# Feed-forward weights loaded by ranges of their 2048 columns, and the second product of two blocks in partial sums

## The chip, the cores and the metric

The kernel runs on one core of a Trainium2 chip. The metric is device time in microseconds (us) of one execution; the time before is the median of three runs. TensorE (PE) does matrix products, VectorE (DVE) and ScalarE (ACT) do elementwise work and read PSUM, GpSimd (POOL) does elementwise work in SBUF, and SyncE (SP) issues all DMAs, in one queue and in order.

## What is computed

Attention with pooled queries, then a gated feed-forward layer:

```python
q_pool = q.reshape(4, 8, 576, 2, 64).mean(axis=3)
attn = softmax(q_pool @ k.T / 8)          # 4 x 8 heads, 576 x 1152
x = (attn @ v), heads side by side        # 2304 rows x 512
h = x @ w_in                              # w_in 512 x 2048
g = h / (1 + exp(-h))
out = g @ w_out                           # w_out 2048 x 512
```

q, k, v, w_in and w_out are float32 (the two weights are handed over in the bit pattern of 64-bit floats, which the kernel turns into float32 by shifts and masks). Each product is done in three float16 products (high by high, high by low, low by high).

## The kernel before

**Jobs.** Attention is cut into 72 jobs, 18 for each of 4 batches: 128 pooled query rows of one pair of heads, or the last 64 rows of two pairs (ch is None). A job is scores (`scores`, L555, PE into the PSUM tiles S0 and S1), row maxima (L602, DVE), exponentials p (L618, ACT), their float16 high and low parts phl (cast L308 or L312, rest L323), a transpose of both by DMA (L641) into pt (or, for one side of the first four jobs, on PE: `turn`, L655), the product with V (`heads`, L700, into the PSUM tile po), and its scaling into x (L746, DVE). An exponential frees its S tile for the next scores.

**Blocks.** When the four pairs of a chunk are done, `rows` transposes x on PE (L771, PSUM tile px; L792 reads it) and `block` does 128 rows of the feed-forward layer; there are 18 blocks. `first(u)`, u = 0 to 3, computes 512 of the 2048 columns of h in 48 matmuls (L833) into a PSUM tile h; tanh (L847, ACT), a multiply-add (L854, DVE, which frees h), a cast and a rest give the float16 pair g[u]. `second` multiplies g by w_out in 48 matmuls (L877), one accumulation over all 16 groups of 128 columns in one PSUM tile o; one evacuation with scaling (L892, by ACT L308 or DVE L314) gives osb, which is stored. Eight g buffers hold two blocks.

**Weights.** `weights(n)`, n = 0 to 31, loads and converts 512 columns' worth of one eighth: n = 0 to 15 are w_in, 16 to 31 w_out. Each is a DMA (L455), a cast of the upper words into a PSUM tile t (ACT L308 or DVE L314, written as `mm<-wide` or `mm<-raw`), three DVE steps (L470, L478, L486, the last one frees t), a cast to the high half (`w`) and a rest to the low half (POOL, L323). The w_in pieces land in a wide SBUF buffer laid over the place where w_out will stand, so the tokens in `staged` make a w_out piece wait for the w_in pieces that lay there; the w_out pieces land in the shared pool b (12 buffers, which also hold loaded q, k, v, p, phl and pt).

**PSUM.** Of the eight banks six are S0 and S1; the tag mm has two buffers (`BUFS["mm"]`), which t, po, pp, px, h and o all share.

**Order.** A planner (`Plan.order`) simulates the engines with a cost for each step and writes out a fixed order for each engine. Attention has priorities near its job's number (the `PRI` offsets), weights near 0.95 + 0.3 n, the feed-forward matmuls 1e6 and more, so that these fill what is left:

```python
pr = 1e6 + 1000 * bid                          # block bid
"pe", 12 * pe_cost(P), lambda i=i: products(i), pr + 10 * u          # first
"pe", pe_cost(DM, DM, DM), lambda ff=ff: products(ff), pr + 100 + ff # second
w2_tokens = [x for u in range(8) for x in weight_tokens("w2", u)]
```

The last of these lines makes every step of `second` wait for the whole of w_out.

Of the kernel before, what the change touches and what calls it, by code (L numbers as in the profile page):

```python
# [53 lines left out]
FIRST_LEAD, FIRST_STEP = 2.2, 1.0  # L54
W_FIRST, W_STEP, W2_LATER = 0.95, 0.3, 0.58
V_LATER = 1.71
PRI = dict(
    score=0.07, top=-1.08, exp=-0.21, hi=0.07, lo=0.0, turn=-3.26, flip=-0.32, flat=-0.7, sums=-0.83,
    rows=0.65, side=0.2, load=-0.59, raw=-1.0,
)  # L60
EARLY, KL_EARLY, T_EARLY, WLO_EARLY, ADD_EARLY = 8, 2, False, True, True
MLP_EVAC, T_EVAC = 4.42, -1.48
BUFS = dict(w=1, slots=4, b=12, x32=2, x4=1, xt=4, g=8, t=4, small=6, S=1, mm=2)
RAW_ROOM, LOAD_ROOM, P32_ROOM, PHL_ROOM = 2, 4, 2, 0
# [5 lines left out]
AHEAD, SWITCH, STEAL = 0.78, 0.82, 1.18  # L70
# [186 lines left out]
def tile_kernel(tc, q, k, v, w_in, w_out, out):  # L257
    nc = tc.nc
    with ExitStack() as ctx:
# [3 lines left out]
        def pool(name, bufs, tags, **kw):  # L263
            pools[name] = ctx.enter_context(tc.tile_pool(name=name, bufs=bufs, **kw))
            for tag in tags:
                capacity[tag] = bufs
# [18 lines left out]
        pool("t", BUFS["t"], ["t"])  # L285
        pool("small", BUFS["small"], ["nm", "sum", "r"])
# [127 lines left out]
        def weights(n):  # L414
            name, src, scale = ("w1", w_in, W_IN_SCALE) if n < 16 else ("w2", w_out, W_OUT_SCALE)
            u, i = divmod(n % 16, 2)
            pr = W_FIRST + W_STEP * n + (W2_LATER if n >= 16 else 0)
            half = f"{name}_{u // 4}"
            if u % 4 == 0 and i == 0:
                wt[name, u // 4] = tile("w", half, [P, 4, 2, 1024], F16)  # L420
            w = wt[name, u // 4]
            if n < 16:
                half, at = n // 4, n % 4
                if at == 0:
                    wide[half] = tile("w", f"w2_{half % 2}", [P, 4, 1024], F32, "wide")
                raw = wide[half]

                def bits():
                    return raw()[:, at]
            else:  # L430
                raw = tile("b", "b", [P, S], F32, "raw", RAW_ROOM)

                def bits():
                    return raw()[:, :1024]
# [58 lines left out]
            if more != 1.0:  # L493
# [5 lines left out]
                x for a in range(2) for x in weight_tokens("w1", 4 + u // 4 * 2 + a)  # L499
# [307 lines left out]
        def block(xt, where, inputs, left=False):  # L807
# [60 lines left out]
            def second():  # L868
                o = tile("psM", "mm", [P, DM], F32)
                osb = tile("t", "t", [P, DM], F32, "osb")  # L870
                tok = ("o", bid)

                def products(ff):
                    u, e = divmod(ff, 2)
                    w = wt["w2", u // 4]()
                    for gl, wl in ((0, 0), (0, 1), (1, 0)):
                        nc.tensor.matmul(  # L877
                            o(), lhsT=g[ff // 4]()[:, gl, ff % 4],
                            rhs=w[:, u % 4, wl, e * DM : e * DM + DM],
                            start=ff == 0 and gl + wl == 0, stop=ff == 15 and gl == 1,  # L880
                        )

                w2_tokens = [x for u in range(8) for x in weight_tokens("w2", u)]
                for ff in range(16):
                    u = ff // 4
                    add(
                        "pe", pe_cost(DM, DM, DM), lambda ff=ff: products(ff), pr + 100 + ff,
                        [("ghi", bid, u), ("glo", bid, u), *w2_tokens], [tok],
                        [o, g[u], wt["w2", ff // 8]],
                    )  # L890
                either(
                    cast(DM, osb, o, 1.0 / (G_SCALE * W_OUT_SCALE)),  # L892
                    MLP_EVAC, [], [tok, ("osb", bid)], [o, osb], port=False,
                )
# [65 lines left out]
```

## Time and profile before

| | |
|---|---|
| three runs | 758.71, 764.72, 764.65 us; median 764.65 us |
| the profiled execution | 758.84 us, of which the profile's span is 757.1 us |
| busy, share of the span | PE 88%, DVE 68%, ACT 61%, POOL 58% |
| granted TensorE clock, mean | 0.96 |

Rows of the trace are given as follows. A row of stretches has its length, then each engine's busy time and its instructions, the granted TensorE clock (1.00 is 2.4 GHz, 0.50 is 1.2 GHz), the busy share of the DMA engines and GB/s. A row of waits names an instruction, what it waited for, the sum in us, how often, and the longest. A row of the timeline has start, length, engine, line, operation and count, and in brackets the idle time of the engine before it and what ended it. Times are us from the start of the span.

### The profile page before, as it was taken

To read this page: it belongs to the slowest core of one execution; us is meant where nothing else is said; L and a number is where in the kernel's file an instruction comes from. 1 tells how busy PE (TensorE), PEld (TensorE's weight loads), DVE (VectorE), ACT (ScalarE), POOL (GpSimd) and SP (SyncE) were. 2 spreads that over 40 slices of the span, in tenths; PEclk is the share of its full clock that TensorE was granted. 3 is DMA by queue.
4 is the path that set the end of the run, shared out by engine and by line. 5 is a ranking of instruction groups with operands and counts; after the bars stand their busy time and mean duration, and the time that the engine had idled before them with its cause. 6 is when DMAs were issued, how large, how long until landed. Compare 5 with 4: busy or idle time off the path is not lost. (4 is left out here: it accounts for less than half of the span.)

```text
span 757.1 us, 23661 instructions
## 1 busy us (share of the span) xinstructions
PE 664.5 (88%) x10188; PEld 478.9 (63%) x10188; DVE 518.4 (68%) x919; ACT 460.1 (61%) x678; POOL 436.7 (58%) x244
## 2 busy tenths in 40 slices
PE   1665736868989999999989999999999999999997
PEld 0343624755575868675956667777767586767874
DVE  5689898877479767766489677677668676666110
ACT  5878866785368556466567556656658465556221
POOL 4847687885126848367546564757626564848111
PEclk9868776999999999999999999999999999999999
DMA  9989988999997999999998999999998997999300
GB/s 306 221 248 241 228 190 176 190 190 175 226 285 143 157 173 150 167 159 186 211 250 172 163 141 153 166 176 205 175 278 145 154 159 151 155 172 149 58 16 14
DMA packets 346024, 133.93 MB, mean 177 GB/s; under 512 B 333376, under 2 KB 333376, under 8 KB 345920
## 3 DMA queue, kind: packets, MB, share of 16 engines
q1 hardware_dynamic: 345920, 132.43, 92.4%
q8 instruction: 79, 1.29, 0.7%
q14 instruction: 25, 0.20, 0.1%
HBM read 45.09 MB, written 4.72 MB: 66 GB/s over the span
## 5 line engine op out<-in xcount | busy, mean ns | idle before, releaser
L323 POOL TENSOR_TENSOR phl<-p,phl 128x1152 f16<-128x1152 f32 x112 | 271.6, 2429 | 153.0 <-DVE phl L312 61.0
L618 ACT ACTIVATE p<-S,nm 128x1152 f32<-128x1152 f32 x144 | 174.5, 1215 | 112.3 <-DVE nm L609 73.8
L833 PE MATMUL mm<-xt,w 128*128 128x128 f16 x3456 | 208.7, 221 | 16.6 <-DVE xt L792 4.3
L833 PEld LDWEIGHTS <-w 128*128 128x128 f16 x3456 | 198.4, 99 | 24.5 <-issue 13.2
L602 DVE TENSOR_REDUCE nm<-S 128x1 f32<-128x1152 f32 x144 | 189.6, 1349 | 30.9 <-PE S L555 30.6
L877 PE MATMUL mm<-w,g 128*128 128x512 f16 x864 | 199.4, 379 | 2.0 <-DVE t L854 0.8
L323 POOL TENSOR_TENSOR g<-t,g 128x512 f16<-128x512 f32 x72 | 93.4, 1301 | 90.6 <-ACT g L308 89.2
L700 PE MATMUL po<-V,pt 128*128 128x64 f16 (+1 forms) x4320 | 132.4, 196 | 13.8 <-DVE t L854 6.3
L700 PEld LDWEIGHTS <-pt 128*128 128x128 f16 (+1 forms) x4320 | 127.7, 103 | 24.5 <-issue 17.5
L877 PEld LDWEIGHTS <-g 128*128 128x128 f16 x864 | 79.9, 98 | 89.2 <-issue 1.9
L555 PE MATMUL S<-KH,QH 64*128 64x512 f16 (+2 forms) x480 | 90.6, 343 | 31.7 <-ACT p L618 23.5
L555 PEld LDWEIGHTS <-QH 64*128 64x128 f16 (+1 forms) x960 | 46.4, 100 | 89.7 <-issue 50.5
L308 ACT ACTIVATE phl<-p 128x1152 f16<-128x1152 f32 x86 | 99.8, 1164 | 4.3 <-issue 2.4
L854 DVE SCALAR_TENSOR_TENSOR t<-t,mm 128x512 f32<-128x512 f32 x72 | 49.2, 684 | 55.0 <-ACT t L847 53.1
L555 PE MATMUL S<-KL,QH 64*128 64x512 f16 (+2 forms) x480 | 85.7, 340 | 0.9 <-DVE KL L323 0.9
L555 PE MATMUL S<-KH,QL 64*128 64x512 f16 (+2 forms) x480 | 79.5, 339 | 0.0
L312 DVE CAST phl<-p 128x1152 f16<-128x1152 f32 x54 | 43.0, 797 | 44.7 <-ACT p L618 41.8
L847 ACT ACTIVATE t<-mm 128x512 f32<-128x512 f32 x72 | 42.6, 594 | 43.7 <-PE mm L833 43.6
L308 ACT ACTIVATE g<-t 128x512 f16<-128x512 f32 x72 | 45.4, 630 | 29.4 <-DVE t L854 29.4
L323 DVE TENSOR_TENSOR phl<-p,phl 128x1152 f16<-128x1152 f32 x28 | 49.5, 1767 | 12.8 <-ACT phl L308 12.4
L323 POOL TENSOR_TENSOR QL<-ld,QH 128x576 f16<-128x576 f32 x15 | 22.9, 1525 | 40.6 <-ACT QH L308 35.8
L746 DVE TENSOR_TENSOR x<-po,r 128x128 f32<-128x128 f32 x72 | 20.4, 284 | 30.2 <-PE po L700 30.0
(48 smaller groups left out, 460.2 us busy)
## 6 DMA issues: line engine op xcount, KB each, us to landing
ld<-v SPq DMA_DIRECT2D x16, 576.0 KB, 8.7
wide<-w_in SPq DMA_DIRECT2D x16, 512.0 KB, 5.8
raw<-w_out SPq DMA_DIRECT2D x16, 512.0 KB, 5.4
ld<-q SPq DMA_DIRECT2D x8, 576.0 KB, 6.1
ld<-k SPq DMA_DIRECT2D x8, 576.0 KB, 7.1
ld<-q SPq DMA_DIRECT2D x16, 288.0 KB, 9.5
ld<-k SPq DMA_DIRECT2D x16, 288.0 KB, 8.5
pt<-phl SPq DMA_TRANSPOSE x280, 3.6
```

The costliest lines, as they stand in the source:

```text
L308: nc.scalar.activation(out=out(), in_=src(), func=AF.Copy, scale=scale or 1.0)
L312: nc.vector.tensor_copy(out=out(), in_=src())
L323: return lambda: getattr(engine, op)(out=out(), in0=a(), in1=b())
L555: nc.tensor.matmul(o[to, c], lhsT=a[pp]()[rows, s], rhs=x[pp]()[rows, c], start=n == 0, stop=n == 2,)
L602: lambda: nc.vector.tensor_reduce(out=nm(), in_=ps()[:, :S], op=ALU.max, axis=AX.X),
L618: lambda: nc.scalar.activation(out=p32(), in_=ps()[:, :S], func=AF.Exp, scale=0.0625, bias=nm(), accum_out=sm()[:, col : col + 1],),
L700: nc.tensor.matmul(o[to, keep], lhsT=pt[:, hl * NK + c, cols], rhs=vv[:, vl, 2 * c + h], start=c == 0 and hl + vl == 0, stop=c == NK - 1 a ...
L746: lambda: nc.vector.tensor_tensor(out=to(), in0=po()[:, : 2 * D].rearrange("p (a d) -> p a d", a=2), in1=r().unsqueeze(2).to_broadcast([P, ...
L833: nc.tensor.matmul(o, lhsT=w[:, f // 2 % 4, wl, cols], rhs=moving(xl, kk), start=kk == 0 and wl + xl == 0, stop=kk == 3 and wl == 1,)
L847: lambda: nc.scalar.activation(out=t(), in_=h(), func=AF.Tanh, scale=1.0 / G_SCALE),
L854: lambda: nc.vector.scalar_tensor_tensor(out=t(), in0=t(), scalar=1.0, in1=h(), op0=ALU.add, op1=ALU.mult,),
L877: nc.tensor.matmul(o(), lhsT=g[ff // 4]()[:, gl, ff % 4], rhs=w[:, u % 4, wl, e * DM : e * DM + DM], start=ff == 0 and gl + wl == 0, stop= ...
```

## The change

The numbering of the weight pieces takes w_in and w_out in turn: pieces 0 to 3 are the first eighth of both, 4 to 7 the second, and so on; pieces 0 to 15 are the first 1024 of the 2048 columns of both weights. The wide landing buffers now lie over the place of the second halves of both, and a piece of a second half waits for all pieces of both first halves (`staged`). The second product of block 0 is done in four parts and that of block 1 in two (`PIECES`): each part has its own PSUM tile, waits only for the eighths of w_out that it uses, and stands among the steps of `first` in priority; the first part is evacuated into an SBUF tile acc, each further one is scaled and added to acc by a DVE step. The other 16 blocks keep the single accumulation. Some 20 constants of the planner are changed as well (priorities, room to be left in the buffers, switching).

```diff
--- before.py
+++ after.py
@@ -51,23 +51,24 @@
 
 WAIT = 0.1
 PREP_LEAD = 3.0
-FIRST_LEAD, FIRST_STEP = 2.2, 1.0
+FIRST_LEAD, FIRST_STEP = 0.91, 1.0
 W_FIRST, W_STEP, W2_LATER = 0.95, 0.3, 0.58
-V_LATER = 1.71
+V_LATER = 1.45
 PRI = dict(
-    score=0.07, top=-1.08, exp=-0.21, hi=0.07, lo=0.0, turn=-3.26, flip=-0.32, flat=-0.7, sums=-0.83,
-    rows=0.65, side=0.2, load=-0.59, raw=-1.0,
+    score=-0.06, top=-1.4, exp=-0.21, hi=0.27, lo=-0.34, turn=-3.17, flip=-0.32, flat=-1.01, sums=-1.89,
+    rows=0.65, side=0.26, load=-0.59, raw=-0.14,
 )
 EARLY, KL_EARLY, T_EARLY, WLO_EARLY, ADD_EARLY = 8, 2, False, True, True
-MLP_EVAC, T_EVAC = 4.42, -1.48
-BUFS = dict(w=1, slots=4, b=12, x32=2, x4=1, xt=4, g=8, t=4, small=6, S=1, mm=2)
-RAW_ROOM, LOAD_ROOM, P32_ROOM, PHL_ROOM = 2, 4, 2, 0
+MLP_EVAC, T_EVAC = 4.42, -0.66
+BUFS = dict(w=1, slots=4, b=12, x32=2, x4=1, xt=4, g=8, t=4, acc=2, small=6, S=1, mm=2)
+RAW_ROOM, LOAD_ROOM, P32_ROOM, PHL_ROOM = 2, 3, 2, 1
+PIECES = 4, 2
 BOTH_BY_PE, ONE_BY_PE, EVERY = 0, 4, 99
 
 
 LATENCY = {"pe": 0.25, "dve": 0.15, "act": 0.15, "pool": 0.15, "dma": 2.2}
 DMA_START = 1.3
-AHEAD, SWITCH, STEAL = 0.78, 0.82, 1.18
+AHEAD, SWITCH, STEAL = 0.91, 0.85, 1.18
 
 
 class Tile:
@@ -283,6 +284,7 @@
         pool("xt", BUFS["xt"], ["xt"])
         pool("g", BUFS["g"], ["g"])
         pool("t", BUFS["t"], ["t"])
+        pool("acc", BUFS["acc"], ["acc"])
         pool("small", BUFS["small"], ["nm", "sum", "r"])
         pool("psS", BUFS["S"], ["S0", "S1"], space=bass.MemoryType.PSUM)
         pool("psM", BUFS["mm"], ["mm"], space=bass.MemoryType.PSUM)
@@ -412,18 +414,17 @@
         wt, wide = {}, {}
 
         def weights(n):
-            name, src, scale = ("w1", w_in, W_IN_SCALE) if n < 16 else ("w2", w_out, W_OUT_SCALE)
-            u, i = divmod(n % 16, 2)
-            pr = W_FIRST + W_STEP * n + (W2_LATER if n >= 16 else 0)
-            half = f"{name}_{u // 4}"
+            u, which, i = n // 4, n // 2 % 2, n % 2
+            name, src, scale = (("w1", w_in, W_IN_SCALE), ("w2", w_out, W_OUT_SCALE))[which]
+            pr = W_FIRST + W_STEP * n + W2_LATER * which
             if u % 4 == 0 and i == 0:
-                wt[name, u // 4] = tile("w", half, [P, 4, 2, 1024], F16)
+                wt[name, u // 4] = tile("w", f"{name}_{u // 4}", [P, 4, 2, 1024], F16)
             w = wt[name, u // 4]
             if n < 16:
-                half, at = n // 4, n % 4
+                space, at = n // 4, n % 4
                 if at == 0:
-                    wide[half] = tile("w", f"w2_{half % 2}", [P, 4, 1024], F32, "wide")
-                raw = wide[half]
+                    wide[space] = tile("w", f"w{space % 2 + 1}_1", [P, 4, 1024], F32, "wide")
+                raw = wide[space]
 
                 def bits():
                     return raw()[:, at]
@@ -496,7 +497,7 @@
                     pr, writes=[("raw", *tok)], tiles=[raw], early=True,
                 )
             staged = [] if n < 16 else [
-                x for a in range(2) for x in weight_tokens("w1", 4 + u // 4 * 2 + a)
+                x for a in range(4) for what in ("w1", "w2") for x in weight_tokens(what, a)
             ]
             either(
                 cast(512, hi, value), pr, [("raw", *tok), *staged], [("whi", *tok)], [raw, w], early=True,
@@ -866,32 +867,51 @@
                 )
 
             def second():
-                o = tile("psM", "mm", [P, DM], F32)
-                osb = tile("t", "t", [P, DM], F32, "osb")
-                tok = ("o", bid)
-
-                def products(ff):
-                    u, e = divmod(ff, 2)
-                    w = wt["w2", u // 4]()
-                    for gl, wl in ((0, 0), (0, 1), (1, 0)):
-                        nc.tensor.matmul(
-                            o(), lhsT=g[ff // 4]()[:, gl, ff % 4],
-                            rhs=w[:, u % 4, wl, e * DM : e * DM + DM],
-                            start=ff == 0 and gl + wl == 0, stop=ff == 15 and gl == 1,
+                n = PIECES[bid] if bid < len(PIECES) else 1
+                scale = 1.0 / (G_SCALE * W_OUT_SCALE)
+                if n == 1:
+                    osb = tile("t", "t", [P, DM], F32, "osb")
+                else:
+                    osb = tile("acc", "acc", [P, DM], F32)
+                for piece in range(n):
+                    ffs = range(16 // n * piece, 16 // n * (piece + 1))
+                    o = tile("psM", "mm", [P, DM], F32)
+                    tok = ("o", bid, piece)
+
+                    def products(ff, o=o, ffs=ffs):
+                        u, e = divmod(ff, 2)
+                        w = wt["w2", u // 4]()
+                        for gl, wl in ((0, 0), (0, 1), (1, 0)):
+                            nc.tensor.matmul(
+                                o(), lhsT=g[ff // 4]()[:, gl, ff % 4],
+                                rhs=w[:, u % 4, wl, e * DM : e * DM + DM],
+                                start=ff == ffs[0] and gl + wl == 0, stop=ff == ffs[-1] and gl == 1,
+                            )
+
+                    w2_tokens = [x for u in {f // 2 for f in ffs} for x in weight_tokens("w2", u)]
+                    at = pr + 100 if n == 1 else pr + 10 * (ffs[-1] // 4) + 5
+                    for ff in ffs:
+                        u = ff // 4
+                        add(
+                            "pe", pe_cost(DM, DM, DM), lambda ff=ff, p=products: p(ff),
+                            at + 0.1 * (ff - ffs[0]),
+                            [("ghi", bid, u), ("glo", bid, u), *w2_tokens], [tok],
+                            [o, g[u], wt["w2", ff // 8]],
                         )
-
-                w2_tokens = [x for u in range(8) for x in weight_tokens("w2", u)]
-                for ff in range(16):
-                    u = ff // 4
-                    add(
-                        "pe", pe_cost(DM, DM, DM), lambda ff=ff: products(ff), pr + 100 + ff,
-                        [("ghi", bid, u), ("glo", bid, u), *w2_tokens], [tok],
-                        [o, g[u], wt["w2", ff // 8]],
-                    )
-                either(
-                    cast(DM, osb, o, 1.0 / (G_SCALE * W_OUT_SCALE)),
-                    MLP_EVAC, [], [tok, ("osb", bid)], [o, osb], port=False,
-                )
+                    if piece == 0:
+                        either(
+                            cast(DM, osb, o, scale),
+                            MLP_EVAC, [], [tok, ("osb", bid)], [o, osb], port=False,
+                        )
+                    else:
+                        add(
+                            "dve", dve_cost(DM),
+                            lambda o=o: nc.vector.scalar_tensor_tensor(
+                                out=osb(), in0=o(), scalar=scale, in1=osb(),
+                                op0=ALU.mult, op1=ALU.add,
+                            ),
+                            MLP_EVAC, [], [tok, ("osb", bid)], [o, osb], port=False,
+                        )
 
                 def store():
                     at = 0
```

## Rows read from the trace of the kernel before

**Rows 1.** Five stretches of the span, all engines.

```profile
0.00:76.00 76.00, 39.24 (x413) 25.31 (x414) 56.85 (x103) 55.57 (x81) 46.16 (x33) 0.84 0.99 254
76.00:176.00 100.00, 64.38 (x1089) 52.11 (x1087) 88.27 (x163) 73.27 (x112) 80.05 (x50) 0.85 0.97 196
176.00:230.00 54.00, 49.14 (x711) 32.83 (x710) 35.04 (x54) 28.25 (x41) 15.53 (x10) 0.97 1.01 221
230.00:700.00 470.00, 459.55 (x7307) 331.51 (x7306) 331.05 (x590) 290.41 (x426) 284.82 (x146) 1.00 1.00 173
700.00:757.00 57.00, 52.21 (x676) 37.18 (x673) 7.20 (x12) 12.59 (x21) 10.10 (x9) 0.98 0.16 30
```

**Rows 2.** The chain that ended last, from 700 us: start, length, what.

```profile
731.13 10.72 PE mm L833 x192
741.85 10.37 PE mm L877 x48
...
752.30 0.60 ACT osb L308
```

**Rows 3.** Waits of PE in the stretch 76 to 176 us.

```profile
PE S L555 <- ACT p L618: 17.0, 5, 10.8
PE po L700 <- DVE t L854: 6.3, 4, 2.1
PE mm L833 <- DVE wide L486: 3.1, 1, 3.1
PE px L771 <- DVE raw L486: 2.5, 1, 2.5
```

**Rows 4.** Timeline of POOL, 90 to 180 us, low halves of the weights.

```profile
95.55 2.47 POOL L323 TENSOR_TENSOR w<-raw,w 128x512 f16<-128x512 f32 x2
...
121.24 1.15 POOL L323 TENSOR_TENSOR w<-wide,w 128x512 f16<-128x512 f32 x1
...
175.84 1.15 POOL L323 TENSOR_TENSOR w<-raw,w 128x512 f16<-128x512 f32 x1
```

**Rows 5.** The same stretches, matmuls of the second product (L877) alone.

```profile
76.00:176.00 100.00, 0.88 (x5) 0.41 (x6) 0.85 0.97 196
176.00:230.00 54.00, 22.81 (x99) 9.04 (x98) 0.97 1.01 221
```

**Rows 6.** Timeline of PE, 94 to 180 us.

```profile
117.62 0.58 PE L555 MATMUL S<-KH,QH 64*128 64x512 f16 x1 [10.76 <-ACT p L618]
...
133.98 1.74 PE L700 MATMUL po<-V,pt 128*128 128x64 f16 x54 [1.41 <-DVE t L854]
...
157.00 2.85 PE L833 MATMUL mm<-xt,w 128*128 128x128 f16 x48
...
165.04 0.65 PE L771 MATMUL px<-one,x 128*128 128x128 f32 x4
```

**Rows 7.** Timeline of DVE, 94 to 180 us.

```profile
99.42 0.67 DVE L486 SCALAR_TENSOR_TENSOR wide<-wide,mm 128x512 uint32<-128x512 uint32 x1
...
135.75 0.29 DVE L746 TENSOR_TENSOR x<-po,r 128x128 f32<-128x128 f32 x1 [0.74 <-PE po L700]
...
160.51 0.69 DVE L854 SCALAR_TENSOR_TENSOR t<-t,mm 128x512 f32<-128x512 f32 x1 [0.65 <-ACT t L847]
```

**Rows 8.** Timeline of ACT, 88 to 128 us.

```profile
94.79 0.65 ACT L308 ACTIVATE mm<-wide 128x512 f32<-128x512 f32 x1
```

**Rows 9.** DVE's groups of instructions in 76 to 176 us: busy, mean ns.

```profile
L478 DVE SCALAR_TENSOR_TENSOR mm<-mm,raw 128x512 uint32<-128x512 uint32 x16 | 11.0, 692 | 1.1 <-ACT mm L308 0.7
...
L854 DVE SCALAR_TENSOR_TENSOR t<-t,mm 128x512 f32<-128x512 f32 x8 | 5.5, 686 | 3.3 <-ACT t L847 3.2
...
L478 DVE SCALAR_TENSOR_TENSOR mm<-mm,wide 128x512 uint32<-128x512 uint32 x7 | 4.8, 690 | 0.1
```

**Rows 10.** Shorter stretches, all engines.

```profile
95.00:114.00 19.00, 5.47 (x76) 3.93 (x74) 18.21 (x28) 11.13 (x16) 15.64 (x11) 0.77 0.84 186
114.00:133.00 19.00, 12.43 (x141) 9.26 (x141) 16.66 (x32) 13.25 (x21) 14.37 (x10) 0.68 0.91 176
```

## The prediction, made before the changed kernel had run

> **What bounds the kernel now.** First the busy shares by stretch [rows 1]. From 230 to 700 us PE works 459.55 of 470 us at a clock of 1.00, while DVE, at 331 us, is the next busiest engine: from there on the end is the sum of PE's work. Before 76 us PE idles 36.8 us, from 76 to 176 us 35.6 us, and from 176 to 230 us 4.9 us. So of the 92.6 us that PE idles, 72.4 lie ahead of 176 us, and only feed-forward work brought forward into them can shorten the whole; what is moved within the later stretches gains nothing. Next the end of the chain that ended last [rows 2]: two blocks of pure PE work, the last one 10.72 us of first product and 10.37 us of second, then an evacuation of 0.60 us. These 21.1 us a block are the unit of what can be moved, and the tail itself stays as it is (blocks 16 and 17 keep one accumulation).
>
> Then, who keeps PE idle between 76 and 176 us [rows 3]: 17.0 us are scores waiting for an exponential to free S (10.8 us in one piece), and the rest is mostly waits for whoever reads a tile of the two mm buffers last: 6.3, 3.1 and 2.5 us in the three largest such rows. Behind both stands DVE, 88.27 us busy of 100 [rows 1], with the weights' bit steps among the attention's. Last, why there is no second product in this stretch: POOL writes the last low half of w_out at 175.84 us [rows 4], and of the 864 matmuls of L877 five stand before 176 us and some hundred in the 54 us after it [rows 5]. Each step of `second` waits for all of w_out, and the eight g buffers, which hold the two blocks that are waiting, keep block 2 from starting.
>
> **The order of the weights.** The DMAs, casts, bit steps and rests are the same 32 pieces, so no engine gets less of them. What moves is what each eighth releases. Pieces 0 to 15 are now both first halves. In the trace of before the last of the first 16 pieces is done at 122.4 us (121.24 plus 1.15) and the last of all at 177.0 [rows 4]. If the pieces keep these times, columns 0 to 1023 of both weights are there by 122 us, and the third quarter (pieces 16 to 23) by about 150, halfway to the end.
>
> **The parts of the second product.** By 176 us the first three quarters of block 0 and the first half of block 1 can then be through: 36 + 24 = 60 matmuls of L877. At 48 in 10.37 us [rows 2] that is 13.0 us of PE work. Against it, `first(3)` of both blocks, which in before was done by 160 us (the last group begins at 157.00 and takes 2.85, rows 6), now needs pieces 24 to 29 and can fall behind 176: 0 to 5.7 us lost. For it the freed g buffers (block 0's first three and block 1's first two) admit block 2, whose x is transposed at 165.04 us [rows 6]: 0 to 8.6 us gained for up to three groups. These two are of the same kind and nearly the same size; I take zero for their sum and keep -5.7 to +8.6.
>
> **PSUM.** Do the parts find one of the two mm buffers free? A tile t is held from its cast at 94.79 to the end of L486 at 100.09, 5.3 us [rows 7, 8]; a tile h from 157.00 to 161.20, 4.2 us [rows 6, 7]; po from 133.98 to 136.04, 2.1 us [rows 6, 7]. From 76 to 176 us there are 16 + 7 of t and 8 of h [rows 9]; nine of po and two of px follow from the nine jobs and two chunks that end in it. With px at po's length that makes 23 x 5.3 + 8 x 4.2 + 11 x 2.1 = 179 of 200 us, an estimate that leaves 21. A part of 12 matmuls takes 2.6 us, and its reader 0.6 to 0.7 (the evacuation of rows 2; an add from PSUM and SBUF of this size is L854's 0.69, rows 9), with the hand-over some 3.6; the part of 24 takes 6.2. Three and one need 17 us. They fit barely, and only in the places where the planner's weights leave a buffer: the long idle piece before 117.62 [rows 6] is just where t's stand back to back. I take 70% of the 13.0 us as moved, 9 us; the bounds are 0 and 13.
>
> **The adds.** Block 0 has three and block 1 one, 4 x 0.69 = 2.8 us of DVE, which has 11.7 us idle of 100 here. The first part's evacuation is the one that was there. They can hold up a row maximum queued behind them on DVE, and with it an exponential and the next scores, by up to 2.8 us in all; PE's order in this stretch has idle time for that, so the cost to the end is 0 to 2.8, and I take 0. Without that idle time it would be the 2.8. The two blocks' stores to HBM follow earlier in SP's queue; the planner gives a store the priority 1e5, behind all of attention's DMAs, so I charge nothing, and without that a transpose behind it would wait for its issue.
>
> **What is late next.** With 9 us fewer of feed-forward work in stock, PE can run dry later. The place is the change of batches, where attention waits for loads of q, k and v; from 230 to 700 us PE idles 10.45 us in all [rows 1], so little is lost there now. As attention's own PE steps stand behind fewer feed-forward steps, it also comes earlier. I charge 1 us, bounds 0 and 5.
>
> **The constants.** Priorities of loads, weights and transposes shift by under two jobs, and the order of every queue with them, SP's included. A plan that is worse after 230 us can cost at most what PE then waits more; one that is better can win at most PE's 10.45 us [rows 1]. I take 0, bounds -5 and +5.
>
> **The sum.** 758.84 - 9 + 1 = 750.8 us on the profiled execution's own time (span 757.1 and 1.7 around it). That execution lies at the low end of the runs shown: their median is 5.8 us higher, and nothing in the trace says which of the two levels the changed kernel's runs will have. I give 752.
>
> **Rival: hidden.** The parts stand in the plan behind every weight step, find no mm buffer, and come out after 176 us; or they run and push back the weights by as much. Then nothing is gained but a shorter hold of o, 0 to 2 us: 757 to 759 on the profile, up to 764 at the level of the median. For it speak rows 3 and the 179 of 200 us; against it, that o's own buffer is free in the same stretch in before and that 35.6 us of PE idle are spread over all of it. The Trainium skill (Perfetto Trace Analysis, Optimization Strategy) reads repeated gaps on the engine that should be saturated as a sign that the next tile finds no room in SBUF or PSUM. The rows of waits on L854 and L486 agree for about a third of the idle time, and the 17.0 us on the exponential do not; by the rule alone this rival's time holds.
>
> **Rival: more.** All 13 us move, block 2 adds half of its 8.6, and PE's clock rises. From 95 to 133 us the granted clock is 0.77 and 0.68 [rows 10], between the two levels of 1.2 and 2.4 GHz, after and among idle stretches of PE. At these means, 46% and 64% of the time lie at the lower level; if its 5.47 and 12.43 us of work are spread alike, full clock would give back half of 2.5 + 8.0, 5 us. Together 13 + 4 + 5 = 22, less 2 for the stock: 738 to 741. Against it is that much of the idle time stays, the exponentials being late.
>
> **Rival: slower.** The new `staged` makes every piece of a second half wait for all of both first halves. In before, the first low halves out of pool b are written at 95.55 us, 25.7 us ahead of the last from the wide buffers [rows 4]. If those pieces now hold their b buffers until the first halves are through, p and phl find none, SP's queue stands with its transposes behind a load that waits for a buffer, and the weights end up to 25.7 us later, at 202. By 202 us PE has done in before the 21.4 us of two first products [rows 2] and some 12 us of second (the 0.88 us ahead of 176 and half of the 22.81 in the 54 us after it, rows 5), 33.7 together. In the changed kernel only first halves would be there: three half first products of 5.4 us and two half second products of 5.2, 26.5 together. The 7.2 us missing, and two jobs of attention held up, each with 1.74 us for po [rows 6] and about as much for its scores, 7 us, give 773, or up to 779 at the level of the median. It decides from the time at which the weights end: at 176 us those 26.5 are 4.2 more than the 22.3 of before, which then gains (11.4 + 7) / 25.7 = 0.7 us in each; so slower than before from about 182 us on. Against it: the first halves come first in every queue, and could be through before 121 if nothing of the second halves stands among them.
>
> **Chances.** Forecast 0.50 (747 to 757), hidden 0.24 (757 to 764), more 0.13 (736 to 745), slower 0.13 (768 to 780). About 1% is what a measurement of this kernel can tell from no change: 7.6 us, so faster is below 757.0, slower above 772.3. Faster: 0.50 + 0.13 = 0.63; within 1%: 0.24 and the lower end of the slower case, 0.26; slower 0.11. The range that holds 8 in 10 takes in the forecast, the hidden case and half of the larger gains, and reaches a little above the hidden case for the new plan's unknown: 740 to 766.
>
> **What would show it.** L877 matmuls in the stretch before 176 us: 60 if the forecast holds, under 15 if hidden. PE's idle time ahead of 176 us falls from 72.4 to about 63 us. The last low half of the weights ends at 170 to 182 us; later than that the slower case is in force. PE's share from 230 to 700 us stays over 97%; under 96% means that stock ran out or that the new order made waits. Waits of po and h on the last reader of an mm tile grow by no more than 5 us. The prediction would be wrong if attention, not PE, set the pace after 230 us, which idle PE at the changes of batches would show, or if the new constants moved the weights as a whole.

## The result, and the profile after

The changed kernel takes 767.25 us (median of 18 runs, 761.22 to 773.10) where the kernel before takes 759.70 us (18 runs, 758.71 to 764.72; the 764.65 known to the prediction came of three): a ratio of 1.009, 95% interval 1.007 to 1.0111. It was forecast at 752 us with a range of 740 to 766; it came out slower than the kernel before, by a little less than the 1% that the prediction takes for the least that can be told from no change. The profiled execution took 766.22 us with a span of 764.5. In its lines L487 is the weights' last DVE step (L486 before), L556 the scores, L701 po, L747 x, L834 the first product, L885 the second, L909 the add; the kernels of the experiments have small shifts of their own.

The five stretches [rows 1], with the last one 7.5 us longer:

```profile
0.00:76.00 76.00, 38.76 (x378) 24.06 (x379) 56.26 (x98) 51.50 (x74) 44.97 (x31) 0.79 0.88 228
76.00:176.00 100.00, 71.22 (x1026) 49.49 (x1026) 88.03 (x163) 70.67 (x105) 66.92 (x40) 0.88 0.99 202
176.00:230.00 54.00, 47.12 (x813) 35.67 (x814) 38.55 (x64) 33.83 (x51) 29.73 (x20) 0.97 1.02 222
230.00:700.00 470.00, 453.27 (x7240) 329.78 (x7237) 334.21 (x582) 285.77 (x421) 274.66 (x142) 1.00 0.98 174
700.00:764.50 64.50, 58.54 (x742) 40.97 (x738) 12.89 (x23) 17.17 (x28) 15.23 (x12) 1.00 0.23 44
```

The second product alone [rows 5]:

```profile
76.00:176.00 100.00, 15.65 (x60) 5.95 (x60) 0.88 0.99 202
176.00:230.00 54.00, 14.43 (x63) 5.92 (x63) 0.97 1.02 222
```

The move took place to the matmul: 60 of L885 stand between 76 and 176 us, as the prediction had it, against 5 before. PE idles 66.0 us ahead of 176 us instead of 72.4. And yet from 230 to 700 us PE idles 16.7 us instead of 10.45, and the end comes later. By the rows of stretches, PE works 511.8 us after 230 us in both kernels; it idles 22.7 us there instead of 15.2, and that difference is the 7.4 us by which the span grew. What else moved is seen in POOL's timeline, the last low half of the weights [rows 4], which ends 32 us later, at 209.1 instead of 177.0:

```profile
207.91 1.16 POOL L325 TENSOR_TENSOR w<-raw,w 128x512 f16<-128x512 f32 x1
```

and in DVE's timeline, where L747 (L746 before) ends a job of attention. Counted in the order in which they end, these are the 13th, 16th, 18th (the last of batch 0), 54th (three batches' worth), 71st and last of the 72 jobs, before:

```profile
168.88 0.29 DVE L746 TENSOR_TENSOR x<-po,r 128x128 f32<-128x128 f32 x1 [0.32 <-PE po L700]
...
192.64 0.28 DVE L746 TENSOR_TENSOR x<-po,r 128x128 f32<-128x128 f32 x1
...
208.09 0.29 DVE L746 TENSOR_TENSOR x<-po,r 128x128 f32<-128x128 f32 x1 [5.69 <-PE po L700]
...
548.64 0.29 DVE L746 TENSOR_TENSOR x<-po,r 128x128 f32<-128x128 f32 x1 [1.39 <-PE po L700]
...
702.96 0.29 DVE L746 TENSOR_TENSOR x<-po,r 128x128 f32<-128x128 f32 x1 [3.12 <-PE po L700]
...
709.76 0.29 DVE L746 TENSOR_TENSOR x<-po,r 128x128 f32<-128x128 f32 x1 [4.40 <-PE po L700]
```

and after:

```profile
161.51 0.28 DVE L747 TENSOR_TENSOR x<-po,r 128x128 f32<-128x128 f32 x1
...
201.10 0.29 DVE L747 TENSOR_TENSOR x<-po,r 128x128 f32<-128x128 f32 x1
...
214.66 0.29 DVE L747 TENSOR_TENSOR x<-po,r 128x128 f32<-128x128 f32 x1 [2.44 <-PE po L701]
...
550.83 0.29 DVE L747 TENSOR_TENSOR x<-po,r 128x128 f32<-128x128 f32 x1 [2.46 <-PE po L701]
...
709.78 0.29 DVE L747 TENSOR_TENSOR x<-po,r 128x128 f32<-128x128 f32 x1 [0.95 <-PE po L701]
...
720.63 0.29 DVE L747 TENSOR_TENSOR x<-po,r 128x128 f32<-128x128 f32 x1 [2.47 <-PE po L701]
```

Attention is 7.4 us ahead at its 13th job, then loses 16 us by the 16th, so that it is 6.6 us late at the end of batch 0. The delay does not stay as it is: 2.2 us after 54 jobs, 6.8 after 71, and 10.9 at the last job, ahead of which the new order puts 84 matmuls of first product (4.7 us on PE). For that the stretch from the last job to the end of the span is 3.5 us shorter (43.9 instead of 47.3 us); 10.9 less 3.5 is the 7.4 us between the spans. This last stretch belongs to the planned order: it is 47.2 to 47.4 us in all eight runs below that keep the order of the kernel before, and 43.9 in all three that keep that of the changed one. Within one order, the end follows attention's last job. The last block is as it was [rows 2]:

```profile
738.70 10.72 PE mm L834 x192
749.42 10.37 PE mm L885 x48
...
759.88 0.60 ACT osb L310
```

PE's waits from 76 to 176 us [rows 3] have changed hands. Two more rows of before that name the weights' last DVE step, which frees a PSUM tile, are these:

```profile
PE po L700 <- DVE wide L486: 1.7, 1, 1.7
...
PE po L700 <- DVE raw L486: 0.6, 1, 0.6
```

and after:

```profile
PE po L701 <- DVE wide L487: 7.2, 1, 7.2
PE mm L885 <- DVE raw L487: 4.9, 3, 2.3
...
PE mm L834 <- DVE t L855: 1.7, 2, 1.5
...
PE po L701 <- DVE t L855: 1.4, 1, 1.4
...
PE S L556 <- ACT p L619: 0.7, 1, 0.7
...
PE mm L885 <- DVE wide L487: 0.5, 1, 0.5
```

The 17.0 us of scores waiting for an exponential have shrunk to 0.7. The PE steps that waited for the weights' last DVE step, attention's po among them, make 12.6 us, where the four rows of this kind before make 7.9. The waits for the multiply-add, which frees the same kind of tile, fell meanwhile, from 6.3 us to 3.1 (L855 after). And the longest of these waits, 7.2 us, ends at 109.9 us, long before attention falls behind. From 161 to 201 us, where it does, PE idles 11.3 us instead of 5.9; the rows of waits there name no single releaser.

### The profile page after: what moved, and what is told of

It is laid out like the page before. It is cut to its first block, busy times and chain, and to the rows that moved or that the text cites. A ratio compares the mean times of both kernels' runs of the same rounds, so it can differ in the third digit from the quotient of the medians.

```text
span 764.5 us, 23652 instructions
## 1 busy us (share of the span) xinstructions
PE 668.9 (87%) x10188; PEld 480.0 (63%) x10188; DVE 530.0 (69%) x926; ACT 458.9 (60%) x676; POOL 431.5 (56%) x243
## 5 line engine op out<-in xcount | busy, mean ns | idle before, releaser
L834 PE MATMUL mm<-xt,w 128*128 128x128 f16 x3456 | 209.6, 220 | 15.9 <-DVE t L855 7.0
L834 PEld LDWEIGHTS <-w 128*128 128x128 f16 x3456 | 198.3, 98 | 23.6 <-issue 18.8
L885 PE MATMUL mm<-w,g 128*128 128x512 f16 x864 | 201.3, 382 | 7.1 <-DVE raw L487 4.9
L701 PE MATMUL po<-V,pt 128*128 128x64 f16 (+1 forms) x4320 | 132.2, 196 | 25.8 <-DVE wide L487 12.7
L701 PEld LDWEIGHTS <-pt 128*128 128x128 f16 (+1 forms) x4320 | 127.9, 103 | 37.3 <-issue 21.8
L325 POOL TENSOR_TENSOR g<-t,g 128x512 f16<-128x512 f32 x72 | 90.8, 1262 | 89.6 <-ACT g L310 87.8
L885 PEld LDWEIGHTS <-g 128*128 128x128 f16 x864 | 80.3, 98 | 95.8 <-issue 6.6
L556 PE MATMUL S<-KH,QH 64*128 64x512 f16 (+2 forms) x480 | 91.0, 349 | 21.9 <-ACT p L619 14.0
L310 ACT ACTIVATE phl<-p 128x1152 f16<-128x1152 f32 x88 | 101.9, 1164 | 1.1
L556 PEld LDWEIGHTS <-QH 64*128 64x128 f16 (+1 forms) x960 | 47.0, 101 | 80.1 <-issue 43.1
L855 DVE SCALAR_TENSOR_TENSOR t<-t,mm 128x512 f32<-128x512 f32 x72 | 49.3, 685 | 58.8 <-ACT t L848 57.4
L556 PE MATMUL S<-KL,QH 64*128 64x512 f16 (+2 forms) x480 | 86.7, 345 | 0.9 <-DVE KL L325 0.9
L556 PE MATMUL S<-KH,QL 64*128 64x512 f16 (+2 forms) x480 | 80.6, 344 | 0.0
L314 DVE CAST phl<-p 128x1152 f16<-128x1152 f32 x52 | 41.1, 789 | 41.2 <-ACT p L619 32.8
L325 DVE TENSOR_TENSOR phl<-p,phl 128x1152 f16<-128x1152 f32 x27 | 51.9, 1924 | 10.3 <-ACT phl L310 10.3
L556 PEld LDWEIGHTS <-QL 64*128 64x128 f16 (+1 forms) x480 | 28.9, 102 | 18.2 <-issue 5.2
L747 DVE TENSOR_TENSOR x<-po,r 128x128 f32<-128x128 f32 x72 | 20.5, 285 | 24.7 <-PE po L701 24.5
```

Source lines behind the costliest of these rows:

```text
L310: nc.scalar.activation(out=out(), in_=src(), func=AF.Copy, scale=scale or 1.0)
L314: nc.vector.tensor_copy(out=out(), in_=src())
L325: return lambda: getattr(engine, op)(out=out(), in0=a(), in1=b())
L556: nc.tensor.matmul(o[to, c], lhsT=a[pp]()[rows, s], rhs=x[pp]()[rows, c], start=n == 0, stop=n == 2,)
L701: nc.tensor.matmul(o[to, keep], lhsT=pt[:, hl * NK + c, cols], rhs=vv[:, vl, 2 * c + h], start=c == 0 and hl + vl == 0, stop=c == NK - 1 a ...
L747: lambda: nc.vector.tensor_tensor(out=to(), in0=po()[:, : 2 * D].rearrange("p (a d) -> p a d", a=2), in1=r().unsqueeze(2).to_broadcast([P, ...
```

## The experiments

Theory A is the prediction's premise: PE's sum of work sets the end. Theory B: attention's chain (scores, maximum, exponential, transposes, product with V) sets it, feed-forward work only fills the gaps, and the change has made attention of batch 0 late, through DVE's time, PSUM, the order of the weights or the planner's constants. Ratios are to the kernel before, with 95% intervals. "Order kept" means that the planned order on the engines is that of the named kernel and only the issued instructions differ; in the other runs the planner writes a new order.

**Does PE's work set the end?** Twice work was taken from PE, order kept, by leaving two of three float16 products out of some second products (the output then lacks them):

```diff
+LIGHT, LIGHT_BLOCKS = ((0, 0),), (0, 1)
...
-                    for gl, wl in ((0, 0), (0, 1), (1, 0)):
+                    for gl, wl in LIGHT if bid in LIGHT_BLOCKS else ((0, 0), (0, 1), (1, 0)):
```

Blocks 0 and 1:

> The kernel before, its order on every engine unchanged, with 64 of the 96 matmuls of the second product of blocks 0 and 1 left out (two of three float16 products): 13.8 us of PE work less between 175 and 211 us, as much as the change was to move ahead of 176. If PE's sum of work sets the end, as the prediction said: 13 us less, 746 to 748 us. If attention's own chain sets the pace from there on and the feed-forward work only fills: 0 to 4 us less, 756 to 760 us.

Measured: 759.42 us, ratio 0.9998 (0.9973 to 1.0022). 13.8 us of PE work less gain nothing. Part of it went to a lower clock, 0.81 granted from 176 to 230 us instead of 0.97, between the two levels, while PE idled more; but from 230 to 700 us the clock is 1.00 in both and PE is as busy as before (459.84 us). The attention steps behind the gap did not come sooner, and the last job of attention is where it was:

```profile
710.17 0.29 DVE L747 TENSOR_TENSOR x<-po,r 128x128 f32<-128x128 f32 x1 [4.40 <-PE po L701]
```

Blocks 9 to 12, in the stretch in which PE is busiest:

> The kernel before, its order on every engine unchanged, with two of the three float16 products of the second product left out in blocks 9 to 12: 27.6 us of PE work less between about 430 and 600 us. If PE's work sets the pace there (97 to 98% busy): 20 us less or more, 740 us. If attention's chain sets it: 0 to 5 us less, 755 to 760 us.

Measured: 763.42 us, ratio 1.0047 (1.0015 to 1.008). One row of stretches of the kernel before and one of this:

```profile
430.00:600.00 170.00, 165.45 (x2632) 118.53 (x2630) 117.94 (x208) 104.56 (x154) 97.67 (x52) 1.00 1.03 178
```

```profile
430.00:600.00 170.00, 145.57 (x2528) 111.44 (x2525) 117.43 (x206) 103.44 (x152) 98.70 (x53) 0.97 1.00 176
```

PE's busy time falls by 20 us in it, the other engines' stays, and the time is not a microsecond less. Theory A falls for the two stretches that were tested. Why this one is 0.5% slower is not known; its last job ends 4.0 us late, and from 560 to 580 us the granted clock is 0.83, between the two levels, where it was 1.00 before.

After 600 us theory A is not tested. There the kernel before shows

```profile
600.00:700.00 100.00, 99.58 (x1662) 73.50 (x1661) 66.76 (x131) 60.88 (x95) 67.73 (x34) 1.00 0.93 156
```

and its chain that ended last runs on PE alone, feed-forward steps included, from 601.5 to 670.9 us and again from 681.1 to 752.2. No run takes work out of this stretch; PE's work may well set its length. Nor does an order that is kept show what a new plan would make of freed time.

**Does the front's DVE time set it?** Two reductions of a constant tile behind L486 of pieces 8 to 31, order kept, which nothing waits for:

```diff
+                if n >= 8:
+                    for _ in range(2):
+                        nc.vector.tensor_reduce(out=spare(), in_=one(), op=ALU.max, axis=AX.X)
```

> The kernel before, its planned order unchanged, with two row maxima of a constant 128 x 128 tile added on DVE behind the last bit step of 24 weight pieces: 48 instructions of about 0.2 us, some 9 us of DVE time between 60 and 175 us that nothing waits for. If DVE's time up to the end of batch 0's attention is what that end and the whole follow: the last job of batch 0 ends 7 to 10 us later, 766 to 769 us. If DVE's idle time there (45 us by then) takes it up: 760 to 762 us.

Measured: 768.97 us, ratio 1.0125 (1.0085 to 1.0166). The 48 reductions took 282 ns each, 13.5 us in all and not some 9. The end of batch 0 and the last job:

```profile
218.05 0.29 DVE L753 TENSOR_TENSOR x<-po,r 128x128 f32<-128x128 f32 x1 [5.69 <-PE po L707]
...
722.18 0.29 DVE L753 TENSOR_TENSOR x<-po,r 128x128 f32<-128x128 f32 x1 [4.40 <-PE po L707]
```

10.0 us late at the end of batch 0, 10.9 after 54 jobs and 12.4 at the last. In the order of the kernel before, a delay of attention in front is carried through to the end, as theory B has it. Forty of the same reductions, 11.3 us, in blocks 4 to 8 (two behind each L854, order kept):

> The kernel before, its order kept, with two row maxima of the constant tile added on DVE behind the multiply-add of blocks 4 to 8: 40 instructions, some 9.5 us of DVE time between 285 and 445 us, where DVE is 70% busy and PE 97%. If DVE's chain sets attention's pace there too: 766 to 769 us. If its idle time takes it up: 759 to 762 us.

Measured: 761.40 us, ratio 1.0024 (0.9994 to 1.0055). There most of it is taken up; in the trace the last job ends 2.6 us late.

**Which part of the change costs?** The new constants alone, the new order alone, the change without the parts (`PIECES = ()`), and the order with the parts under the old constants:

> The kernel before with the planner's new constants alone (old order of the weights, no parts). If the constants are the cause: 766 us or more. If the order of the weights is: 758 to 762 us, with the weights' end back near 177 us.

> The kernel before with the new order of the weights alone (old constants, second products whole). If the order is what costs (weights or attention of batch 0 later): 766 us or more, above the 763.8 of the kernel with the parts under old constants. If the parts and the feed-forward work that they bring forward are what costs, by their DVE time: 758 to 761 us.

> The changed kernel with the second products of blocks 0 and 1 whole again (order of the weights and constants stay new). If the parts themselves cost the time (adds on DVE, PSUM tiles taken from the weights), this is near the kernel before, 760 us, or below it. If the order of the weights or the constants cost it, it stays at 766 us or goes above, since the second products then wait for the weights' end at about 209 us.

> The kernel before with the new order of the weights and the parts, under the old constants. If the structure is the cause (a second half waits for both first halves): 765 us or more, with the weights' end past 190 us. If the new constants are the cause: 750 to 756 us, as was forecast.

| ratio | old constants | new constants |
|---|---|---|
| old order | 1 | 1.0157 (1.0111 to 1.0204) |
| new order | 1.040 (1.0358 to 1.0442) | 1.0234 (1.0196 to 1.0272) |
| new order and parts | 1.005 (1.0023 to 1.0077) | 1.009 (1.007 to 1.0111) |

In medians, 759.75 and 773.25 us in the first row (758.92 for the runs beside the new order alone), 790.64 and 778.03, 763.83 and 767.25. Each cell is a plan of its own, so the columns do not add up: the order costs 4.0% under the old constants and 0.8% on top of the new ones, the parts give 3.5% and 1.4% back, and the constants, which cost 1.6% on their own, add 0.4% to order and parts. All five changed cells lie above 1. Of the two times that were expected for the order alone, the lower one, 758 to 761, did not come. Nor does the late end of the weights go with the cost: the last low half ends at 193.9 us with the constants alone and with the order alone, and at 181.5 with order and parts under the old constants, where batch 0 still ends 7.7 us late and the time stays above the 750 to 756 that was expected if the new constants were the cause. In the trace of the order alone PE, whose queue is in order, stands once for 9.9 us before a first product, with attention's steps behind it (waits from 126 to 180 us):

```profile
PE mm L834 <- DVE raw L487: 9.9, 1, 9.9
```

**The coarse wait** (all sixteen pieces of the first halves before any second half) cut to the pieces that really lie there, planned anew:

```diff
-                x for a in range(4) for what in ("w1", "w2") for x in weight_tokens(what, a)
+                x for a in (which, which + 2) for what in ("w1", "w2") for x in weight_tokens(what, a)
```

> The changed kernel with the wait of the second halves cut to the pieces whose landing buffers really lie there (half of the first sixteen each), planned anew. If that wait is what costs (the weights end at 209 us instead of 177): weights' end near 190 us or earlier and 758 to 763 us. If not: 765 to 770 us.

Measured: 772.59 us, ratio 1.0206 (1.0159 to 1.0252), above both times that were expected. The weights still end at 204.8 us, and the plan is another one, so this clears the coarse wait only in part.

**The adds**, each issued four times:

> The changed kernel, its order kept, with each of the four adds of partial sums issued four times (the sum is then wrong by the repeats): 12 instructions of 0.65 us more on DVE, 7.8 us, between about 130 and 215 us. If the front's DVE time is what the change pays with: 4 to 8 us more than the changed kernel, 771 to 775 us. If DVE's idle time takes the adds up, as the prediction had it: 766 to 769 us.

Measured: 769.78 us, ratio 1.0147 (1.011 to 1.0184), 2.5 us over the changed kernel by the medians and 4.3 by the ratios, for 8 us of DVE. That lies between the two expectations, and the profiled execution (764.59 us) was no slower than the changed kernel's. If the cost goes in proportion, an estimate, the four adds of the change themselves, 2.7 us, cost some 1 us.

**The weights' cast on ACT.** Bound to ACT and planned anew:

> The kernel before with the weights' cast into PSUM bound to ACT (15 of the 32 were on DVE, 9.8 us), planned anew. If DVE's time in front sets the end: batch 0's attention ends 5 to 10 us earlier, 750 to 756 us. If not, or if ACT's casts come later and the weights with them: 760 us or more.

Measured: 786.64 us, ratio 1.0347 (1.0304 to 1.039). It is in the upper of the two ranges expected, but far above what 10 us of casts could cost: the new plan moves more than the cast. Therefore with the order kept, the casts that the plan gives to DVE issued on ACT:

```diff
-                cast(512, t, value, 2.0**-111),
+                [(e, c, t_by_act) for e, c, _ in cast(512, t, value, 2.0**-111)],
```

> The kernel before with its planned order kept as it is and the 15 weight casts that the plan gives to DVE issued on ACT instead, at the same place of the order: 9.8 us of DVE time less up to the end of batch 0, 8.4 us of ACT more (ACT idles 66 us there). If DVE's time in front sets the end: the last job of batch 0 and the whole 6 to 10 us earlier, 749 to 753 us. If it does not, or if the casts on ACT come late and hold DVE up: 757 us or more.

> The same edit on the changed kernel, whose plan gives 21 weight casts to DVE (13.5 us): order kept, casts on ACT. If the changed kernel is late because its front has more DVE time (5.2 us more than before): 755 to 760 us, 8 to 12 us under the changed kernel. If it is late for another reason (order of the weights, parts): 764 us or more.

> The same edit on the kernel with the new order of the weights and the parts under the old constants (18 casts on DVE, 11.9 us). DVE's time as the cause: 752 to 757 us. Otherwise 762 us or more.

Measured: 756.46 us, ratio 0.9957 (0.9932 to 0.9982), faster than both kernels; 762.84 us, 1.0034 (1.0004 to 1.0064), against 1.009 without the edit; and 765.69 us, 1.0069 (1.0038 to 1.0101), no gain. The first two lie between the two times that were expected of them. In the changed kernel batch 0 then ends 4.2 us earlier:

```profile
210.44 0.29 DVE L750 TENSOR_TENSOR x<-po,r 128x128 f32<-128x128 f32 x1 [1.99 <-PE po L704]
```

But in that trace the last job ends only 1.0 us earlier (719.65 us), and this execution, 765.31 us, was only 0.9 us faster than the changed kernel's: there the delay of batch 0 does not come through to the end one to one. DVE's time is worth something in the first two, about a third of a microsecond for one, and no more in the changed kernel than the larger number of casts would explain.

**PSUM.** The weights' tile t in SBUF, order kept, so that two buffers of PSUM are left to the products:

```diff
-            t = tile("psM", "mm", [P, 512], F32)
+            t = tile("tw", "mm", [P, 512], F32, "tw")
```

> The changed kernel, its planned order kept, with the weights' tile t in an SBUF buffer of its own (two of them) in place of the two mm buffers of PSUM; to make room one xt and one g buffer that the plan never uses are left out. PE's and the other engines' instructions are the same. If the two PSUM buffers hold the front up (in the changed kernel 27.6 of 28.8 us of PE's waits from 76 to 176 us end with a reader of an mm tile): 755 to 761 us, 6 us or more under the changed kernel. If not, or if L478 and L486 lose as much to POOL when both their inputs are in SBUF: 765 us or more.

> The same edit on the kernel before (there about half of PE's waits from 76 to 176 us end with a reader of an mm tile). If PSUM is what the change pays with, this gains less than the edit gains on the changed kernel: 755 to 760 us. If DVE's own time sets the front in both: no gain in either, 758 to 762 us.

(The 27.6 us in the first of these count too much: waits for xt and for row maxima are among them. The rows above that name the weights' last step or the multiply-add make 15.7, and their like before 14.2.) Measured: 786.89 us, ratio 1.036 (1.0328 to 1.0392), and 789.35 us, 1.0374 (1.0343 to 1.0406). Inconclusive, because the two DVE steps became dearer (first kernel, 0 to 230 us):

```profile
L490 DVE SCALAR_TENSOR_TENSOR raw<-raw,tw 128x512 uint32<-128x512 uint32 x16 | 26.1, 1634 | 0.2
L482 DVE SCALAR_TENSOR_TENSOR tw<-tw,raw 128x512 uint32<-128x512 uint32 x16 | 22.4, 1400 | 0.3
```

1634 and 1400 ns, where L478 took 692 [rows 9] and L486, the like of L490, 681. The changed kernel lost 20 us by it and the one before 30, which would fit PSUM being tighter in the changed one; it is not shown.

**What sets attention's pace after 230 us?** For batch 2, in the order of the kernel before, 44% less transposing by DMA (PE reads the same five blocks again), and the row maximum over 640 of 1152 columns (so exponentials are shifted by another maximum):

> The kernel before, its order kept; for jobs 36 to 53 (batch 2, about 384 to 540 us) the DMA transposes move 5 of 9 blocks of 128 columns, and the product with V reads the five blocks that are there again in place of the four left out (as many matmuls as before). 44% less transposing over 170 us. If the DMA queue sets attention's pace in that stretch: 15 us less or more, 745 us or below. If not: 757 to 761 us.

> The kernel before, its order kept; for jobs 36 to 53 the row maximum is taken over 640 of the 1152 columns: about 0.55 us less in each of 36, 20 us of DVE time, all of it in the chain scores, maximum, exponential, next scores. If that chain, with one pair of S tiles, sets attention's pace there: 8 to 15 us less, 745 to 751 us. If not: 757 to 761 us.

Measured: 757.77 us, ratio 0.9989 (0.9965 to 1.0014): not the transposes in the DMA queue, whose busy share fell (384 to 540 us, before and here):

```profile
384.00:540.00 156.00, 150.32 (x2325) 107.09 (x2323) 115.36 (x203) 97.49 (x144) 95.33 (x49) 1.00 1.03 174
```

```profile
384.00:540.00 156.00, 150.54 (x2354) 109.99 (x2352) 113.54 (x202) 97.17 (x144) 96.72 (x50) 0.99 0.64 110
```

And 754.90 us, 0.9947 (0.9924 to 0.9971), between the two expectations: some 4 us of the 19 taken out of the chain of scores, maximum and exponential come through. That chain has a share in the pace; what holds the rest stays open.

## Why the prediction was wrong, step by step

**The step that failed** is the first: "from there on the end is the sum of PE's work". It was read from 98% busy, and on it stands the price at which moved work was put, one microsecond of the end for each. 13.8 us less of that work between 175 and 211 us, as much as was to be moved, and 27.6 us less between 430 and 600 gained nothing. The feed-forward matmuls stand there in the gaps that attention's steps leave; taken out, they leave the gaps. After 600 us the premise may hold; no run shows it either way. The Trainium skill (Perfetto Trace Analysis, Identifying the Most-Contended Engine) says that the busy share of matmuls is a poor measure of how near TensorE is to its limit, and names the weight loads as one of the better ones. These stood at 331.5 of 470 us here (PEld, the second figure of [rows 1]); that taking work out gained nothing fits.

**The sum.** "9 us moved" was 70% of the 13.0, though the prediction's own sign for it, 60 matmuls, is all of the 13.0; and 60 moved. They were busy for 15.65 us, at a mean granted clock of 0.88. Against them, 96 matmuls of first product fell behind 176 us (288 of L834 stand before it, where before had 384 of L833), 5.4 us at the price of [rows 2], net of what block 2 gained: the term that was taken as zero. So 6.4 us of PE's idle time ahead of 176 us were used, not 9. At 230 us the changed kernel has done 123 second-product matmuls where before had done 104, and yet PE's work after that is the same 511.8 us: attention has more of its own left. The worth of the move, put at one to one, is about nothing. "What is late next", charged at 1 us with bounds of 0 and 5, looked for stock that runs out on PE; what came was 7.4 us more idle PE after 230 us, with attention late.

**The adds at 0** were right within 1 us or so, by the estimate above. **PSUM**: all parts found a buffer, though 21 of 200 us were thought to be free. Its price in waits on the last reader grew from 14.2 to 15.7 us in the rows on the weights' last step and the multiply-add, within the 5 us that the prediction allowed.

**The order of the weights at no cost** was wrong: "if the pieces keep these times" did not hold, the last came 32 us later, and the table gives the order 4.0% under the old constants and 0.8% on top of the new. **The constants at 0, between -5 and +5**: 3.4 us by the medians on top of order and parts, at the edge of what the runs resolve, and 13.5 alone.

**The rivals.** "Slower" (768 to 780) had its sign, its mark, the weights' end past 182 us, and came nearest in size; but its mechanism did not come about. By 202 us the changed kernel has done 448 matmuls of first product and 60 of second, before 384 and 74, 38 and 37 us at the prices of [rows 2], so no feed-forward work is missing there. Nor did the loads of weights wait longer in SP's queue: from 76 to 215 us 6.2 us instead of 6.8. That its size nearly fits is luck. "Hidden" (757 to 764) failed, since the parts did move. What would have shown the premise wrong was named, attention setting the pace after 230 us, with idle PE as its sign; but PE's share there was 97.8% before and 96.4% after, which does not tell the two apart.

**Left open**: why the changed kernel is slower. Its batch 0 loses its time between 161 and 201 us, and through which of PE's queue, the PSUM buffers, DVE's time and the weights that are still being converted there is not shown. Nor is it shown how much of the 7.4 us comes from batch 0, since the delay is down to 2.2 us after 54 jobs, and how much from the new plan of batch 3.

## What to carry to other kernels

An engine that is 98% busy with filler need not be the bound: take some of its work away with the order kept, stretch by stretch, and see whether the end moves, before moving work is priced at one to one. Ask which chain the filler stands beside, here attention's, and what the moved work takes from that chain in the stretch into which it is moved. Where a planner writes the order, judge an edit's parts with the order kept; planned anew, a set of some 20 constants moved this kernel by 1.6%, and binding one cast to an engine by 3.5%.

## What the hardware showed

The in-place shift of the weights on DVE (L470, 128x512) took 0.42 us with POOL at rest and up to 1.38 us beside POOL; its 16 instructions on `raw` sum to 14.0 us before and, in the kernel with the order alone, to 17.2 (from 0 to 230 us). In the changed kernel they sum to 12.4, so this is not what makes it late. These are the rows of the kernel before and of the one with the order alone:

```profile
L470 DVE TENSOR_SCALAR raw<-raw 128x512 uint32<-128x512 uint32 x16 | 14.0, 878 | 0.0
```

```profile
L471 DVE TENSOR_SCALAR raw<-raw 128x512 uint32<-128x512 uint32 x16 | 17.2, 1090 | 0.0
```

Three rows from DVE's timeline of the kernel before: one with POOL at rest, then two neighbours beside the two POOL instructions that begin at 95.55 us [rows 4], the first shift while one of them ended and the second while the next ran, which ended at 98.02 us:

```profile
38.39 0.42 DVE L470 TENSOR_SCALAR wide<-wide 128x512 uint32<-128x512 uint32 x1
...
96.42 0.59 DVE L470 TENSOR_SCALAR wide<-wide 128x512 uint32<-128x512 uint32 x1
96.93 1.38 DVE L470 TENSOR_SCALAR raw<-raw 128x512 uint32<-128x512 uint32 x1
```

The step with two inputs took 692 ns with one of them in PSUM [rows 9] and 1400 on average with both in SBUF. It is not SBUF as such that is slow: in the changed kernel with the tile in SBUF, five of the 16 instructions `raw<-raw,tw` had no POOL instruction beside them and took 0.68 to 0.70 us, and the other eleven, beside POOL, took 1.44 to 2.75 us. The Trainium skill (SBUF — State Buffer, Who interferes with whom) has VectorE share a port pair with GpSimd, which one of them locks against the other, when VectorE reads two tensors from SBUF while GpSimd reads it too, or runs in a two-port mode. The times of the step with two inputs agree with it, and so do those of the shift, if it runs in such a mode, which no trace here tells. So PSUM tiles for elementwise work on DVE buy time beside a busy POOL, at the price of the two buffers.
